# Loading attention keys through GpSimd's DMA queue, with the cast to float16 made by the transfer

## The chip, the cores and the metric

One core of one Trainium2 chip runs the kernel. The metric is the device time of one execution in microseconds (us); lower is better. The engines are named as the profile names them: PE (TensorE, matrix work; PEld is its weight load), DVE (VectorE), ACT (ScalarE), POOL (GpSimd) and SP (SyncE, which here only issues transfers).

## The reference, cut to what matters

Retention over 8 batches and 8 heads, sequences of 576, head width 64, followed by one feed-forward layer with a gated soft maximum and a normalisation. Inputs and outputs are float32.

```python
scores = scale * np.matmul(q, k.transpose(0, 1, 3, 2))
gamma = 1.0 - 2.0 ** (-5.0 - np.arange(H))
Dmat = np.where(rel >= 0, gamma[:, None, None] ** rel[None], 0.0)
x = np.matmul(scores * Dmat[None], v)        # then heads side by side: 4608 x 512

h = x @ w_in                                 # 4608 x 1024
solu = h * softmax(h)
ln = (solu - mean(solu)) / np.sqrt(var(solu) + 1e-06) * g_ln
out = ln @ w_out                             # 4608 x 512
```

## The kernel before, in words

*Tiling.* The 4608 rows are cut into 36 chunks of 128 rows. Two batches make a group of nine chunks: four of 128 rows of each batch, in turn, and one "tail" that holds the last 64 rows of both (lines 124 to 129; `rows`, line 131). There are four such groups. A chunk has its q, k and v for all eight heads, a tile of 128 x 8 x 64 each.

*Steps of a chunk.* Each is a short function whose name stands in the order. `ld` (line 168) loads q, k and v from memory as float32, on SP's queue: one transfer each of 256 KB, or two of 128 KB for a tail. A transfer gathers runs of 64 elements (256 B), one for each row and head. `cq` and `cv` multiply q and v by powers of gamma and write float16 (`scaled`, line 179). `ck` (line 190) casts the keys to float16 without scaling. For chunks under 15 and for tails `tq` (line 198) transposes q and k on PE; for the others q goes through PE (`tr`, line 217) and k through a transposing transfer on SP's queue (`kd`, line 209, issued at 213). `eq` and `er` copy the transposed tiles out of PSUM. `sc` forms the scores (line 247), `mk` masks them (DVE, line 265), `kv` multiplies keys by values (line 276) and is the last to read the float16 keys, `ad` adds that to the running state (DVE, lines 289 and 291), `dk` and `d3` scale the state to float16 and float32 for the next chunk (POOL, lines 303 and 315), `av` and `fs` form the retention's output (lines 327 and 342), `ex` copies it to float16. The second half is `m1` (first layer, line 374), `mx`, `xp`, `so` (maximum, exponential, gated product: lines 384, 390, 399), `sq` and `rt` (sum of squares on ACT, and the inverse root on POOL in three small instructions, lines 439 to 449), `tu` and `eu` (transpose and copy), `m2` (second layer, line 472) and `st` (ACT scales by the root, line 480, and SP stores, line 485).

*Order.* It is written out by hand. Every engine works through its own instructions in the order in which the steps stand in three lists: START (chunks' first steps, weight loads and weight casts), LOOP, run for i from 7 to 31 with steps at offsets from chunk i, and END. A letter at the end of a step names its engine: g for POOL, v for DVE, a for ACT. A transfer stands in the order of the queue that issues it. In LOOP POOL's steps are, in order, `dk:0`, `cv:3`, `rt:-2`, `cq:4`, `d3:0` and `ck:5`; `ld:6` stands ahead of `dk:0`, and `kd:4` between `dk:0` and `cv:3`. The loop's `ld` therefore covers chunks 13 to 35; START holds those of chunks 0 to 12 (in the order 0, 1, 2, 4, 3, 5 and on). Of the 36 key casts 29 are POOL's, 6 ACT's and 1 DVE's.

*Buffers.* The float32 tiles rotate through 6 buffers for keys and 7 each for q and v, the float16 keys through 6, float16 q and v through 5 each. A step that writes a buffer waits until the last reader of its former content is done.

Of the kernel before, what the change touches and what calls it, by code (L numbers as in the profile page):

```python
# [10 lines left out]
FP = mybir.dt.float32  # L11
F16 = mybir.dt.float16
BF16 = mybir.dt.bfloat16
P = 128
H = 8
D = 64
# [73 lines left out]
def kernel(  # L90
# [10 lines left out]
    nc = tc.nc  # L101
# [11 lines left out]
    load = ctx.enter_context(tc.tile_pool(name="load", bufs=6))  # L113
    half = ctx.enter_context(tc.tile_pool(name="half", bufs=4))
# [16 lines left out]
    def rows(n):  # L131

        bs, c = chunks[n]
        if c < 4:
            return [(slice(0, P), bs[0], c * P)]
        return [(slice(64 * i, 64 * i + 64), b, 4 * P) for i, b in enumerate(bs)]
# [24 lines left out]
    ENG = {"a": nc.scalar, "v": nc.vector, "g": nc.gpsimd}  # L161
    T = {}

    def copy(engine, out, in_):
        (engine.copy if engine is nc.scalar else engine.tensor_copy)(out=out, in_=in_)  # L165


    def ld(n):

        for key, src in (("qf", q), ("kf", k), ("vf", v)):  # L170
            dst = load.tile([P, H, D], FP, name=key, bufs=6 if key == "kf" else 7)
            for pp, b, s0 in rows(n):
                m = pp.stop - pp.start
                nc.sync.dma_start(  # L174
                    out=dst[pp], in_=src[b, :, s0 : s0 + m, :].rearrange("h p d -> p h d")
                )
            T[key, n] = dst
# [10 lines left out]
        scaled(n, "qf", "q16", gqt if chunks[n][1] == 4 else gq, ENG[e])  # L188

    def ck(n, e="g"):  # L190
        k16 = half.tile([P, H, D], F16, name="k16", bufs=6)
        copy(ENG[e], k16, T.pop(("kf", n)))
        T["k16", n] = k16

    def cv(n, e="g"):
        scaled(n, "vf", "v16", gkt if chunks[n][1] == 4 else gk, ENG[e])
# [520 lines left out]
```

## Time and profile before

| What | Value |
|---|---|
| Median of 2 runs | 221.14 us (220.74 to 221.54) |
| The profiled execution's own time | 220.91 us |
| Its span in the profile | 219.1 us |
| Granted PE clock | 0.996 |
| POOL key casts (line 165) | 29, 18.3 us busy, 629 ns mean |
| ACT key casts | 6, 626 ns mean |
| Key loads | 32 of 256 KB, 4.9 us to landing; 8 of 128 KB, 3.7 us |
| Transposing transfers of keys | 18, 3.8 us to landing |
| Data read from memory | 32.70 MB |

The span runs from the first to the last record; the execution's time is a little longer. "Busy" is the time in which an engine has an instruction in work; register, branch and transfer-issuing instructions are not counted in it. In the 40 slices a digit is the busy share of one slice in tenths. The DMA share is the mean busy share of the core's 16 DMA engines. In the table of windows the columns are: the stretch, its length, the busy time of PE, PEld, DVE, ACT and POOL with the number of their instructions, the granted PE clock, the DMA share and GB/s.

### The profile page before, as it was taken

The numbers are of one execution on the slowest core, as the hardware profiler recorded it, in microseconds if no ns is written. First come the engines' busy times: TensorE is split into PE (matmuls) and PEld (weight loads), VectorE is DVE, ScalarE is ACT, GpSimd is POOL, SyncE is SP. The second block draws the span as 40 slices with busy tenths as digits, with TensorE's granted clock in tenths as the row PEclk, the third lists the DMA queues.
The fourth block names the chain that finished last, engine by engine and source line by source line (L and its number), as shares of the span: only waits on it lengthen the run. The fifth ranks groups of instructions, "written<-read, shape, count | busy, mean of one in ns | idle before, by whom it ended". The sixth has DMA issues, their size and how long they took to land.

```text
span 219.1 us, 5479 instructions
## 1 busy us (share of the span) xinstructions
PE 200.1 (91%) x2060; PEld 114.3 (52%) x2060; DVE 174.4 (80%) x285; ACT 170.6 (78%) x274; POOL 174.5 (80%) x272
## 2 busy tenths in 40 slices
PE   1259889999989999999999999999999999999993
PEld 0235455555545555555555555555555555555552
DVE  1178999999997888888877788888878888889940
ACT  2064797989878888888888888888887888897992
POOL 0319899699796899999987899999988999994321
PEclk9999999999999999999999999999999999999998
DMA  7999999999999996799999998899999996610124
GB/s 143 236 282 314 206 221 355 225 203 231 278 279 215 252 205 140 176 253 209 235 236 220 230 219 180 195 247 232 226 226 230 211 226 146 161 51 15 37 97 144
DMA packets 130875, 44.86 MB, mean 205 GB/s; under 512 B 124448, under 2 KB 124832, under 8 KB 130848
## 3 DMA queue, kind: packets, MB, share of 16 engines
q1 hardware_dynamic: 129216, 44.18, 92.1%
q10 hardware_dynamic: 1632, 0.32, 0.9%
q8 instruction: 16, 0.26, 0.6%
q14 instruction: 11, 0.09, 0.2%
HBM read 32.70 MB, written 9.44 MB: 192 GB/s over the span
## 4 chain that ended last, share of the span: by engine, by line
PE 70%; DVE 12%; SPq 12%; DMA 2%; issue 2%; POOL 1%; DVEq 0%; POOLq 0%
PE o L472 24%; PE h L374 21%; SPq L174 10%; PE lp L457 6%; PE sc L252 4%; PE x L342 3%; PE x L327 3%; PE kp L276 3%; DMA qf<-in_q_dram 2%; DVE u L399 2%; DVE nm L384 2%; DVE w_c L669 2%; PE tr L223 2%; DVE ret L265 2%; PE tp L204 2%
## 5 line engine op out<-in xcount | busy, mean ns | idle before, releaser
L374 PE MATMUL h<-w_in,xT 128*128 128x512 f16 x264 | 62.4, 379 | 0.5 <-DVE u L399 0.5
L472 PE MATMUL o<-w_c,uT 128*128 128x512 f16 x232 | 54.6, 379 | 0.2
L390 ACT ACTIVATE e<-h,nm 128x1024 f32<-128x1024 f32 x35 | 39.1, 1116 | 12.5 <-DVE nm L384 12.5
L265 DVE TENSOR_TENSOR ret<-sc,tris 128x512 f16<-128x512 f32 x72 | 46.0, 680 | 0.6 <-PE sc L252 0.6
L399 DVE SCALAR_TENSOR_TENSOR u<-h,e 128x1024 f16<-128x1024 f32 x35 | 42.7, 1220 | 2.5 <-ACT e L390 0.9
L384 DVE TENSOR_REDUCE nm<-h 128x1 f32<-128x1024 f32 x35 | 42.3, 1214 | 1.4 <-PE h L374 1.1
L472 PEld LDWEIGHTS <-uT 128*128 128x128 f16 x280 | 26.1, 98 | 26.3
L374 PEld LDWEIGHTS <-xT 128*128 128x128 f16 x264 | 24.3, 98 | 24.2 <-issue 0.5
L303 POOL TENSOR_TENSOR s<-t,small 128x512 f16<-128x512 f32 x32 | 34.0, 1062 | 3.5 <-DVE t L291 3.5
L181 POOL TENSOR_TENSOR v<-vf,small 128x512 f16<-128x512 f32 x32 | 33.4, 1045 | 3.0 <-DMA vf<-in_v_dram 2.9
L181 POOL TENSOR_TENSOR q<-qf,small 128x512 f16<-128x512 f32 x32 | 33.4, 1044 | 2.8 <-DMA qf<-in_q_dram 2.8
L427 ACT ACTIVATE sq<-u,su 128x1024 bf16<-128x1024 f16 x29 | 33.6, 1159 | 1.0 <-DVE u L399 1.0
L165 ACT CAST xT<-x 128x512 f16<-128x512 f32 x35 | 20.5, 587 | 14.4 <-PE x L342 14.0
L165 ACT COPY uT<-lp 128x1024 f16<-128x1024 f16 x29 | 29.3, 1012 | 0.7 <-PE lp L457 0.4
L480 ACT ACTIVATE o_sb<-o,rs 128x512 f32<-128x512 f32 x35 | 23.8, 683 | 1.0 <-POOL q L181 0.8
L165 POOL CAST k<-kf 128x512 f16<-128x512 f32 x29 | 18.3, 629 | 6.1 <-DMA kf<-in_k_dram 6.1
L449 POOL TENSOR_TENSOR rs<-w,mhalf 128x1 f32<-128x1 f32 x36 | 19.9, 553 | 3.0
L291 DVE TENSOR_TENSOR t<-kp,s 128x256 f32<-128x256 f32 x24 | 10.1, 421 | 15.0 <-POOL s L303 11.8
L457 PE MATMUL lp<-ident,u 128*128 128x128 f16 x280 | 21.3, 219 | 0.7 <-DVE u L415 0.7
L445 POOL TENSOR_SCALAR w<-ss,w 128x1 f32<-128x1 f32 x30 | 8.0, 267 | 13.7 <-ACT sq L427 11.5
L457 PEld LDWEIGHTS <-u 128*128 128x128 f16 x280 | 17.2, 98 | 2.1 <-DVE u L415 0.8
L165 ACT COPY qkT<-tp 128x1024 f16<-128x1024 f16 x10 | 10.0, 1012 | 10.0 <-PE tp L204 10.0
(78 smaller groups left out, 266.3 us busy)
## 6 DMA issues: line engine op xcount, KB each, us to landing
qf<-in_q_dram SPq DMA_DIRECT2D x32, 256.0 KB, 4.4
kf<-in_k_dram SPq DMA_DIRECT2D x32, 256.0 KB, 4.9
vf<-in_v_dram SPq DMA_DIRECT2D x32, 256.0 KB, 4.9
out_dram<-o_sb SPq DMA_DIRECT2D x32, 256.0 KB, 2.9
w_in<-in_moe_w_in_dram SPq DMA_DIRECT2D x4, 512.0 KB, 5.2
w_out<-in_moe_w_out_dram SPq DMA_DIRECT2D x4, 512.0 KB, 6.3
qf<-in_q_dram SPq DMA_DIRECT2D x8, 128.0 KB, 3.4
kf<-in_k_dram SPq DMA_DIRECT2D x8, 128.0 KB, 3.7
```

Source lines behind the costliest of these rows:

```text
L165: (engine.copy if engine is nc.scalar else engine.tensor_copy)(out=out, in_=in_)
L181: engine.tensor_tensor(out=dst, in0=T.pop((key, n)), in1=table.unsqueeze(2).to_broadcast([P, H, D]), op=ALU.mult,)
L265: nc.vector.tensor_tensor(out=r, in0=s, in1=m, op=ALU.mult)
L303: nc.gpsimd.tensor_tensor(out=s16, in0=t.unsqueeze(2).to_broadcast([P, 4, 2, D]), in1=gd.unsqueeze(3).to_broadcast([P, 4, 2, D]), op=ALU.mult,
L374: nc.tensor.matmul(out=h[:, i * 512 : (i + 1) * 512], lhsT=xT[:, d], rhs=w_in16[:, d, i * 512 : (i + 1) * 512], start=d == 0, stop=d == 3,)
L384: nc.vector.tensor_reduce(out=nm, in_=T["h", n], axis=AX.X, op=ALU.max, negate=True)
L390: nc.scalar.activation(out=e, in_=T["h", n], func=ACT.Exp, bias=T.pop(("nm", n)), accum_out=s)
L399: nc.vector.scalar_tensor_tensor(out=u, in0=T.pop(("h", n)), scalar=-1.0, in1=T.pop(("e", n)), op0=ALU.mult, op1=ALU.mult, accum_out=su,)
L427: nc.scalar.activation(out=s, in_=T.pop(("v", n)), func=ACT.Square, scale=-float(DFF), bias=T.pop(("su", n)), accum_out=ss,)
L457: nc.tensor.transpose(out=lp[:, c], in_=u[:, c * P : (c + 1) * P], identity=ident)
L472: nc.tensor.matmul(out=o, lhsT=uT[:, c], rhs=w[:, c], start=c == 0, stop=c == NF - 1)
L480: nc.scalar.activation(out=o_sb, in_=T.pop(("o", n)), func=ACT.Copy, scale=T.pop(("rs", n)))
```

## The change

The keys are loaded by transfers that POOL issues, with a float16 tile as the destination: the transfer itself casts. `ld` stands in the three lists where it stood, so POOL issues a chunk's key load at the place of `ld` in its own order, and SP issues q and v. The float32 key tiles fall away, and `ck` only hands the tile on: it issues nothing. The float16 keys have 14 buffers in place of 6. The orders themselves are the same.

```diff
@@ def ld(n): @@
         for key, src in (("qf", q), ("kf", k), ("vf", v)):
-            dst = load.tile([P, H, D], FP, name=key, bufs=6 if key == "kf" else 7)
+            if key == "kf":
+                dst = half.tile([P, H, D], F16, name="k16", bufs=14)
+                queue = nc.gpsimd
+            else:
+                dst = load.tile([P, H, D], FP, name=key, bufs=7)
+                queue = nc.sync
             for pp, b, s0 in rows(n):
                 m = pp.stop - pp.start
-                nc.sync.dma_start(
+                queue.dma_start(
                     out=dst[pp], in_=src[b, :, s0 : s0 + m, :].rearrange("h p d -> p h d")
                 )
             T[key, n] = dst
@@ def ck(n, e="g"): @@
-        k16 = half.tile([P, H, D], F16, name="k16", bufs=6)
-        copy(ENG[e], k16, T.pop(("kf", n)))
-        T["k16", n] = k16
+        T["k16", n] = T.pop(("kf", n))
```

## The prediction

> **What bounds the kernel now.** I read the page first: busy shares, then the slices.
>
> ```profile
> PE 200.1 (91%) x2060; PEld 114.3 (52%) x2060; DVE 174.4 (80%) x285; ACT 170.6 (78%) x274; POOL 174.5 (80%) x272
> ...
> PE   1259889999989999999999999999999999999993
> ...
> POOL 0319899699796899999987899999988999994321
> ```
>
> PE is full from a third of the way on, POOL nearly so. The table of windows splits this (PE and POOL busy, the DMA share, GB/s at the end).
>
> ```profile
> 0.00:27.00 27.00, 14.76 (x145) 8.74 (x146) 14.93 (x27) 10.76 (x16) 12.36 (x21) 1.00 1.09 236
> 27.00:40.00 13.00, 11.49 (x158) 7.37 (x156) 12.38 (x21) 11.13 (x18) 10.80 (x13) 1.00 1.20 291
> 40.00:62.00 22.00, 21.22 (x176) 11.13 (x175) 21.89 (x39) 19.86 (x32) 19.50 (x29) 1.00 1.05 230
> 120.00:150.00 30.00, 29.97 (x325) 16.97 (x323) 24.68 (x41) 25.12 (x42) 28.36 (x45) 1.00 1.07 220
> ```
>
> Before 27 us no engine is full and transfers set the pace; up to 62 us DVE does; after it PE is busy 29.97 of 30 us. The chain of waits agrees: SP's issues up to 27 us, DVE's work from 34.9 to 62, PE's from there on. In it the first-layer matmul (line 374) starts at 65.85 and at 186.96 with 23 steps between, 121.1 us or 5.27 us a step.
>
> What matters for this change is how little POOL has to spare beside that PE. Its timeline in one full step, start and duration first:
>
> ```profile
> 130.93 1.04 POOL L181 TENSOR_TENSOR v<-vf,small 128x512 f16<-128x512 f32 x1
> 131.95 0.27 POOL L439 TENSOR_SCALAR w<-s 128x1 f32<-128x1 f32 x1
> 132.32 0.27 POOL L445 TENSOR_SCALAR w<-ss,w 128x1 f32<-128x1 f32 x1
> 132.67 0.55 POOL L449 TENSOR_TENSOR rs<-w,mhalf 128x1 f32<-128x1 f32 x1
> 133.19 1.04 POOL L181 TENSOR_TENSOR q<-qf,small 128x512 f16<-128x512 f32 x1
> 134.19 0.61 POOL L315 TENSOR_TENSOR s<-t,small 128x256 f32<-128x256 f32 x1
> 134.75 0.61 POOL L165 CAST k<-kf 128x512 f16<-128x512 f32 x1
> 135.32 1.04 POOL L303 TENSOR_TENSOR s<-t,small 128x512 f16<-128x512 f32 x1
> 136.32 1.04 POOL L181 TENSOR_TENSOR v<-vf,small 128x512 f16<-128x512 f32 x1
> ```
>
> From v to v it is 5.39 us with no wait shown. Start to start the parts are v 1.02, the root's three 1.24, q 1.00, s32 0.56, key cast 0.57, s16 1.00. In the 121.1 us there are 23 v, q and roots, 20 s16, 16 s32 and 22 casts: 23 x 3.26 + 20.0 + 9.0 + 12.5 = 116.5 us. POOL's slack is 4.6 us, 0.2 us a step.
>
> **The change, part by part.** Call X the time POOL spends on issuing one key load of 1024 runs of 256 B.
>
> *Removed casts.* 29 on POOL (0.57 us each), 6 on ACT (0.63), 1 on DVE (0.42). Those on ACT and DVE lie ahead of 62 us beside transfers or DVE's work; I cost them at nothing (below that, at most 4 us in all, if ACT were the bound there; at 19.86 of 22 us it isn't). Those in the loop give POOL 12.5 us, which alone shortens nothing since PE is full.
>
> *Added issues on POOL.* 36 chunks, 32 of one DMA and 4 of two halves (64 partitions each): 40 instructions. In START 13 chunks are loaded, seven of them (0 to 6) queued ahead of what POOL does at 22.8 us, six (7 to 12) after it; the loop loads the other 23, three of them in halves. In the loop the load stands after s32 and ahead of s16, where the cast stood, so X takes the place of 0.57 us: no other step changes its place. Behind it on POOL is s16, for which PE's state matmuls (line 342) wait in the same step, then v, the root (ACT's output scaling waits for it, line 480) and q.
>
> No row shows X. Lower end: SP issues the same load in 0.43 us when nothing holds it. Upper end: POOL's two-input loop takes 1045 ns for 512 elements, 2.04 ns a turn; 1024 reads and then 1024 writes listed one after the other at that rate are 4.2 us. The list is made by POOL's software, so I take the row nearest to it, POOL's simplest loop: the cast's 611 ns for 512 elements is 1.19 ns a turn, 1024 turns are 1.22 us, and one small instruction (0.2 us, line 443) makes X = 1.42; a pair of halves is X + 0.2.
>
> *Loop.* 116.5 - 12.5 + 23 X + 0.6 = 104.6 + 23 X against 121.1: growth 23 X - 16.5, from X = 0.72 on. At 1.42 it is 16.2 us. When POOL is late, s16 is late next, and PE stands still ahead of its state matmuls.
>
> *From 27 to 62 us.* POOL is busy 30.3 of 35 us, 4.7 free. Six chunks' loads, 6 X + 0.2, less two casts (1.1): growth 6 X - 5.6 where positive, 2.9 us at 1.42. DVE, the bound there, waits for POOL's states (lines 289 to 291), so I count it in full; the lower end is 0.
>
> *Up to 27 us.* 7 X less three casts (1.7) in 14.6 us free: growth 7 X - 16.3, nothing at 1.42.
>
> *SP's queue.* 40 issues leave. In the loop it waits for others anyway (30.1 us for ACT's output tiles alone), so nothing there. On the chain before 27 us the key loads are six pieces: 0.57 + 2.25 + 0.78 + 0.91 + 2.52 + 0.91 = 7.9 us. Between 0 and -7.9 I take 0: the packets are still carried, by engines whose share is 1.09 in that window, and the pieces of 2 us and more are waits for them.
>
> *The transfers.* Keys keep their reads; 128 B instead of 256 B are written per run. The queue's line:
>
> ```profile
> q1 hardware_dynamic: 129216, 44.18, 92.1%
> ```
>
> Keys are 36 x 1024 = 36,864 of these packets, 28.5%. If a casting packet took twice the time on engines that are full, the 121.1 us would grow by 34.5. Lower end 0, since less written can't help where PE is the bound. I take 0: the same engines carried 236 and 291 GB/s in the first two windows, and 220 in the loop.
>
> *Added waits.* The key tiles' 14 buffers: the load of chunk n reuses that of n - 14, whose last reader (line 276) ran many steps earlier; no wait. The transposing DMA of keys (line 213) waits for the landing instead of the cast. Its load was issued two steps earlier, 10.5 us, and key loads land after 4.9 us: 5.6 us of cover. Without it SP would stand still with q, v and stores queued behind, and each us of delay past the cover would come back as late q for POOL.
>
> *Contention.* POOL's rows in the loop have the same duration in every step (1.04, 0.61), with DVE at 82%: nothing stretches them. If each load waited for DVE's one wide copy of a step (420 ns, line 165 from PSUM), it would be 23 x 0.42 = 9.7 us more; if none, 0, which I take. The Trainium skill (SBUF — State Buffer, section SBUF: two separate sides, its box on the "DVE blocks DMA" trap) speaks against the change here: POOL can't write descriptors while DVE runs in a mode that takes both ports. By that rule the sum would be 249.4 if the copy is such an instruction; the steady rows don't show such a lock on POOL's own work.
>
> **The sum.** Span 219.1 + 16.2 + 2.9 = 238.2. The profiled execution took 220.91, 1.8 more than its span; so 240.0 us, against a median of 221.14 of two runs, which the profiled one stands 0.2 below.
>
> **The rivals.**
> *Cheap issue.* X under 0.91: the growth (23 X - 16.5) stays within 4.4 us, 2%, which is about what a measurement can tell from no change. PE still sets the loop, and the time is 221 to 225. For it: SP's 0.43 us. Against it: POOL's software loops are the dearest per element in the groups. The Trainium skill (DMA: Bandwidth & Descriptors, section Anatomy of one DMA — SWDGE (gpsimd) path) calls descriptor generation small and says that many can be emitted before the cost shows; by that the sum stays at 221. No run here shows it.
> *Dear issue.* X over 2.3: 23 X - 16.5 + 6 X - 5.6 + 7 X - 16.3; at 2.3 that is 36.4 + 8.2 = 44.6, 265.5 us; at 3.2 it is 57.1 + 13.6 + 6.1, 297.7; at 4.2, 80.1 + 19.6 + 13.1, 333.7. For it: two lists. Against it: two-input work is not what POOL has here.
> *Casting transfers become the bound.* 220.9 + 34.5 = 255.4 with packets of twice the time and a cheap issue. For it: shares of 1.0 to 1.1. Against it: the GB/s above.
> *Faster.* SP's 7.9 us of key issues leave the chain, and q and v land earlier: 213.0. It decides if X is under 0.72 and if issuing, not carrying, paces the first 27 us. Against it: the share of 1.09 there.
> That the keys are not cast on the way is not possible: the tile has another type than the source.
>
> **How the numbers follow.** Forecast (X from 0.91 to 2.3, 225 to 266, likeliest 240.0): 0.46. Dear issue 0.16, transfers 0.10, cheap issue 0.20, faster 0.08. So slower by over 2% 0.72, within 0.20, faster 0.08. The range is 219 to 297: it leaves out the fast case (0.08) and X over 3.2 (0.08).
>
> **What would show it.** Right: POOL without gaps from 62 us on with key loads of 1.2 to 1.6 us between s32 and s16, PE's idle before line 342 or 252 put down to POOL, steps near 5.95 us. Cheap: steps of 5.27 us and POOL with 0.2 us or more free. Transfers: SP's issues of q and v lengthen and POOL waits for qf. Faster: line 374 starts its steady run well before 65.85. Wrong above all if X is not near 1.4, since each 0.1 us is worth 2.9 us.

## The result, and the profile after

The changed kernel takes 233.17 us (median of 232.63 and 233.71) against 221.14: 1.0535 times as long, with a 95% interval from 1.0495 to 1.0574. It is slower. (Executions of a kernel that lie over 1.5% above its fastest count as slow and are left out of such ratios.) The profiled execution took 233.71 us with a span of 231.9.

The page's busy line, two of the slices, the queues and the key loads' own group, after:

```profile
PE 204.9 (88%) x2060; PEld 116.3 (50%) x2060; DVE 179.6 (77%) x284; ACT 168.2 (73%) x268; POOL 194.3 (84%) x283
...
PE   1368787796999999999979999999979999999993
...
POOL 4359999999747999999999999999999999995411
...
q1 hardware_dynamic: 91712, 34.74, 70.7%
q0 software_dynamic: 37504, 4.72, 32.0%
...
L179 POOL DMA_DIRECT2D k<-in_k_dram x40 | 36.7, 917 | 0.8 <-POOLq L704 0.8
```

PE's row of nines has gaps now, and POOL's has hardly any. The issues count as POOL's busy time here: 36.7 us in place of 18.3 us of casts. A second queue carries the keys: 4.72 MB, half the bytes, as float16.

POOL's timeline in a full step of the loop (the root's three small instructions left out):

```profile
129.37 1.05 POOL L186 TENSOR_TENSOR v<-vf,small 128x512 f16<-128x512 f32 x1
...
131.65 1.04 POOL L186 TENSOR_TENSOR q<-qf,small 128x512 f16<-128x512 f32 x1
132.65 0.60 POOL L318 TENSOR_TENSOR s<-t,small 128x256 f32<-128x256 f32 x1
133.21 0.97 POOL L179 DMA_DIRECT2D k<-in_k_dram  x1
134.21 1.06 POOL L306 TENSOR_TENSOR s<-t,small 128x512 f16<-128x512 f32 x1
135.21 1.04 POOL L186 TENSOR_TENSOR v<-vf,small 128x512 f16<-128x512 f32 x1
```

X, the time POOL spends on issuing one key load, is 0.97 us, and start to start 1.00 us where the cast took 0.57. From v to v it is 5.84 us, 0.45 more than before, while PE needs 5.27. A tail's pair of halves, at 139.05, takes 1.45 us.

Where the time went is read from the starts of the 35 exponentials (ACT's line 390, after it 393), one for each row block, in both traces:

| Exponential (counted from 0) | Before, us | After, us | Later by |
|---|---|---|---|
| 3 | 36.89 | 36.94 | 0.05 |
| 4 | 45.00 | 48.12 | 3.12 |
| 6 | 56.98 | 64.54 | 7.56 |
| 7 | 63.74 | 70.63 | 6.89 |
| 14 | 101.64 | 108.53 | 6.89 |
| 16 | 111.97 | 120.84 | 8.87 |
| 25 | 159.09 | 171.16 | 12.07 |
| 34 | 205.55 | 218.27 | 12.72 |

Two losses: 6.9 us between 37 and 70 us, in START, and 5.8 us in the loop after that. The first 37 us have neither gained nor lost. In the loop the loss comes in jumps (14 to 16, 21 to 25): POOL falls 0.45 us behind in each full step until its lead is used up, and catches up in the tails. Who waits there is told by the waits of the changed kernel from 66 to 219 us (in all, times, longest):

```profile
ACT o_sb L483 <- POOL rs L452: 11.4, 11, 1.5
DVE t L294 <- POOL s L318: 10.4, 10, 1.4
```

Only the first of the two is new. Before, ACT never waits for the root in the loop, while DVE waits just as long for POOL's states (10.8 us for line 303 between 62 and 207 us) and nothing is lost by it.

START's loss shows first on DVE. Its centering of u in place (SBUF to SBUF, line 415, now 418), its scaling of q and the centering of w_out that follows, before:

```profile
37.54 1.25 DVE L415 TENSOR_SCALAR u<-u,nmu 128x1024 f16<-128x1024 f16 x1
...
46.10 0.68 DVE L181 TENSOR_TENSOR q<-qf,small 128x512 f16<-128x512 f32 x1
46.71 1.08 DVE L669 TENSOR_TENSOR w_c<-w_out,warm 128x512 f16<-128x512 f16 x3
```

and after:

```profile
38.31 2.90 DVE L418 TENSOR_SCALAR u<-u,nmu 128x1024 f16<-128x1024 f16 x1
...
50.82 2.20 DVE L186 TENSOR_TENSOR q<-qf,small 128x512 f16<-128x512 f32 x1
52.94 2.04 DVE L672 TENSOR_TENSOR w_c<-w_out,warm 128x512 f16<-128x512 f16 x3
```

POOL's timeline after, beside the first of these, shows what stood there in the meantime:

```profile
37.88 0.97 POOL L179 DMA_DIRECT2D k<-in_k_dram  x1
38.88 2.04 POOL L653 TENSOR_TENSOR w_out<-w_out,g 128x512 f16<-128x512 f32 x2
40.86 1.42 POOL L179 DMA_DIRECT2D k<-in_k_dram  x2
```

DVE's centering ends (41.21) just after POOL's two casts of w_out (40.92). Before, POOL's three casts of w_out (37.47, 39.95 and 41.38) each waited for w_out to land, 2.2 us in all, and these waits were pauses beside DVE. In the changed kernel SP issues w_out 1.3 us earlier (29.42 against 30.68), and POOL waits for none of it. So the pauses were closed by two things, POOL's issues and the earlier w_out, and no run separates them.

Then PE, which waits for the centered u, runs slower: the window from 40 to 62 us has a granted clock of 0.84, and the first-layer matmuls that start at 42.74 take 2.96 us instead of 1.89.

Who waits for whom from 27 to 71 us in the changed kernel: ACT waits 0.6 us once for POOL's s16, and that is the only wait for POOL. No engine but POOL itself (0.2 us, for a v) waits for a transfer. DVE is busy for 32.4 of the 35 us from 27 to 62: it stands inside its own instructions.

### The profile page after: what moved, and what is told of

It reads as the page before. It is cut to its first block, busy times and chain, and to the rows that moved or that the text cites. A ratio compares the mean times of both kernels' runs of the same rounds, so it can differ in the third digit from the quotient of the medians.

```text
span 231.9 us, 5465 instructions
## 1 busy us (share of the span) xinstructions
PE 204.9 (88%) x2060; PEld 116.3 (50%) x2060; DVE 179.6 (77%) x284; ACT 168.2 (73%) x268; POOL 194.3 (84%) x283
## 3 DMA queue, kind: packets, MB, share of 16 engines
q0 software_dynamic: 37504, 4.72, 32.0%
## 4 chain that ended last, share of the span: by engine, by line
PE 47%; POOL 22%; DVE 10%; DMA 7%; issue 7%; SPq 3%; ACT 3%; POOLq 0%; DVEq 0%
PE o L475 15%; PE h L377 15%; DMA vf<-in_v_dram 5%; PE lp L460 4%; POOL k L179 4%; POOL v L186 4%; POOL s L306 3%; POOL q L186 3%; POOL s L318 3%; DVE nm L387 3%; PE sc L255 2%; PE x L345 2%; DVE u L402 2%; POOL rs L452 2%; SPq L179 2%
## 5 line engine op out<-in xcount | busy, mean ns | idle before, releaser
L377 PE MATMUL h<-w_in,xT 128*128 128x512 f16 x264 | 65.0, 391 | 0.5 <-DVE u L402 0.5
L393 ACT ACTIVATE e<-h,nm 128x1024 f32<-128x1024 f32 x35 | 39.0, 1115 | 15.6 <-DVE nm L387 15.4
L377 PEld LDWEIGHTS <-xT 128*128 128x128 f16 x264 | 25.0, 100 | 25.5 <-issue 3.0
L179 POOL DMA_DIRECT2D k<-in_k_dram x40 | 36.7, 917 | 0.8 <-POOLq L704 0.8
L186 POOL TENSOR_TENSOR v<-vf,small 128x512 f16<-128x512 f32 x32 | 34.0, 1063 | 2.5 <-DMA vf<-in_v_dram 2.4
L483 ACT ACTIVATE o_sb<-o,rs 128x512 f32<-128x512 f32 x35 | 23.9, 686 | 13.2 <-POOL rs L452 11.4
L165 ACT CAST xT<-x 128x512 f16<-128x512 f32 x35 | 20.5, 585 | 10.5 <-PE x L345 8.7
L294 DVE TENSOR_TENSOR t<-kp,s 128x256 f32<-128x256 f32 x24 | 10.1, 422 | 17.3 <-POOL s L318 10.4
L255 PE MATMUL sc<-qkT 64*128 64x128 f16 x288 | 15.8, 225 | 5.0 <-ACT uT L165 2.3
```

The source lines that it names most:

```text
L179: queue.dma_start(out=dst[pp], in_=src[b, :, s0 : s0 + m, :].rearrange("h p d -> p h d"))
L186: engine.tensor_tensor(out=dst, in0=T.pop((key, n)), in1=table.unsqueeze(2).to_broadcast([P, H, D]), op=ALU.mult,)
L377: nc.tensor.matmul(out=h[:, i * 512 : (i + 1) * 512], lhsT=xT[:, d], rhs=w_in16[:, d, i * 512 : (i + 1) * 512], start=d == 0, stop=d == 3,)
L393: nc.scalar.activation(out=e, in_=T["h", n], func=ACT.Exp, bias=T.pop(("nm", n)), accum_out=s)
```

## The experiments

**How they are read.** Several of these kernels scatter from execution to execution (four of the first experiment took 225.8 to 233.2 us, while the kernel before stayed between 220.97 and 222.39 beside them), so the losses are also read from each profile, which is one execution: START's is how much later exponential 7 starts than before, the loop's is what is added until exponential 34. "DVE's 22" is the busy time of DVE's 22 instructions in START that go from SBUF to SBUF (centering, q, v, w_out, and the centering of w_out, lines 415, 181, 645 and 669 before), the time in which two of one kind overlap counted once. An instruction of these is called held where it takes longer than it does alone.

| Kernel | Median (lowest to highest), us | START loss | Loop loss | DVE's 22, us |
|---|---|---|---|---|
| before | 221.14 (220.74 to 221.54) | 0 | 0 | 14.9 |
| changed | 233.17 (232.63 to 233.71) | 6.9 | 5.8 | 19.6 |
| e1 START only | 231.00 (225.83 to 233.20) | 8.1 | 0.0 | 20.9 |
| e2 loop only | 227.60 (226.95 to 228.09) | 0.7 | 5.9 | 14.8 |
| e3 no cast by the transfer | 248.47 (one run) | 7.4 | 20.0 | 19.4 |
| e4 two loads later | 231.63 (229.22 to 233.86) | 7.0 | 5.8 | 17.7 |
| e5 filler on PE | 234.47 (233.42 to 238.73) | 6.7 | 5.9 | 21.5 |
| e7 pairs | 227.77 (227.44 to 228.36) | 6.1 | 0.8 | 15.5 |
| e8 pairs, w_out on ACT | 228.19 (227.89 to 228.50) | 6.6 | 0.8 | 15.4 |
| e10 START before, pairs in loop | 222.95 (222.18 to 226.86) | 0.3 | 0.8 | 14.6 |
| e11 w_out on ACT | 232.54 (232.13 to 233.28) | 6.3 | 5.8 | 18.7 |
| e12 before, POOL filled | 235.76 (233.13 to 236.77) | 15.5 | 0.2 | 13.2 |

The ratios to before, with their 95% intervals (none for e1 and e3): e2 1.0267 (1.0226 to 1.0307), e4 1.036 (1.0313 to 1.0408), e5 1.0566 (1.0509 to 1.0623), e7 1.0286 (1.0243 to 1.0328), e8 1.0302 (1.0271 to 1.0333), e10 1.0052 (1.0022 to 1.0082), e11 1.0478 (1.0433 to 1.0523), e12 1.0573 (1.0505 to 1.0641).

**e1 and e2: each half of the change alone.** In `ld` and `ck` the new way holds for some chunks only:

```diff
-            if key == "kf":
+            if key == "kf" and n < 13:        # e2: n >= 13
                 dst = half.tile([P, H, D], F16, name="k16", bufs=14)
                 queue = nc.gpsimd
+            elif key == "kf":
+                dst = load.tile([P, H, D], FP, name=key, bufs=6)
+                queue = nc.sync
```

> Chunks 0 to 12 (the START list) get their keys by POOL's casting transfers as in the changed kernel; chunks 13 to 35 (the loop) as before: SP loads float32, the cast is a step of its own. Theory (two separate losses, 7.0 us up to the loop and 5.8 us in it, as the starts of the exponential show them in the two traces): about 228 us, with the loop's steps at 5.27 us. Rival (one loss: POOL is behind from START on, or casting transfers slow all others): either under 224 or as slow as the changed kernel, 233.

> The reverse: chunks 0 to 12 as before, chunks 13 to 35 by POOL's casting transfers. Theory: POOL's time in the loop is the loss, 104.6 + 20 x 0.97 + 3 x 1.42 against 121.1 us gives 7.2 at most, so 227 to 228 us. Rival (POOL only falls behind because it enters the loop late; with a loop entered on time its buffers carry it): under 224 us.

e2 came to 227.6 us, as expected, and lost 5.9 us in the loop after entering it only 0.7 us late; e1 lost nothing at all in its loop, and its four executions lie on both sides of the 228 us expected. So the losses are separate and, within START's scatter, add up: 6.9 and 5.8 in the changed kernel, 8.1 and 0.0 in e1, 0.7 and 5.9 in e2. The rival that POOL is late in the loop only because it enters late has fallen.

**e3: the issue without the cast.** The 36 casts stay, and POOL issues plain float32 loads:

```diff
             if key == "kf":
-                dst = half.tile([P, H, D], F16, name="k16", bufs=14)
+                dst = load.tile([P, H, D], FP, name=key, bufs=6)
                 queue = nc.gpsimd
```

> POOL issues the key loads where the changed kernel does, but as plain float32 into float32 tiles, and the 36 key casts stay where they were before. Theory (POOL's time is the loss in the loop; the issue costs 0.97 us with or without a cast): POOL needs 116.5 + 20 x 0.97 + 3 x 1.42 = 140.2 us for the 23 steps against 121.1, so about 19 us lost in the loop, with START's loss about 247 us. Rival (it is the casting that makes the issue dear, a plain one costs 0.5 us): POOL needs 129 us, 236 us. Rival (casting transfers slow the others, not POOL): no more than 233 us.

248.47 us in its one execution, against 247 expected by the theory. POOL's timeline has the cast and, behind it, an issue at the same price as with casting:

```profile
152.40 0.60 POOL L165 CAST k<-kf 128x512 f16<-128x512 f32 x1
152.95 0.97 POOL L179 DMA_DIRECT2D kf<-in_k_dram  x1
153.95 1.05 POOL L308 TENSOR_TENSOR s<-t,small 128x512 f16<-128x512 f32 x1
```

By POOL's count the loop should lose 116.5 + 20 x 0.97 + 3 x 1.42 - 121.1 = 19.1 us; it lost 20.0. POOL's time is what the loop pays for, and casting has no part in the price.

**e6: the costs by themselves.** A kernel of its own, which leaves out all that the reference computes: DVE and POOL run short rows of the kernel's instructions, alone and side by side.

> No part of the reference is computed (the output is zeros): the disputed costs alone, in stretches that DVE and POOL start together. DVE runs rows of 10 centering steps (128x1024 float16, SBUF to SBUF), 8 scalings of q (two SBUF inputs), 8 copies from PSUM; first alone, then beside 8 casting key loads issued by POOL, then the first two beside 8 scalings by POOL; after that POOL issues key loads of 128, 256, 512 and 1024 runs with the cast and 1024 without. Theory: centering takes 0.49 us alone and about 1 us or more beside either kind of POOL work, scaling 0.68 and over 1.2 us, the copies from PSUM 0.68 in both; the issue takes 0.45 us and 0.5 us for each 1024 runs (0.51, 0.57, 0.70, 0.97). Rival on holding: DVE waits only for POOL's scalings, which read SBUF, and not for issues. Rival on the price: the issue costs the same for any number of runs, or less without the cast.

DVE's rows, in order: 10 centerings and 8 scalings alone, then beside 8 issues, then beside 8 scalings by POOL (8 copies from PSUM, left out here, took 4.87 us alone and 4.86 beside issues):

```profile
9.23 4.05 DVE L130 TENSOR_SCALAR u<-u,scal 128x1024 f16<-128x1024 f16 x10
13.83 4.90 DVE L135 TENSOR_TENSOR o<-qf,table 128x512 f16<-128x512 f32 x8
...
24.70 5.25 DVE L130 TENSOR_SCALAR u<-u,scal 128x1024 f16<-128x1024 f16 x10
33.67 4.90 DVE L135 TENSOR_TENSOR o<-qf,table 128x512 f16<-128x512 f32 x8
...
49.33 10.32 DVE L130 TENSOR_SCALAR u<-u,scal 128x1024 f16<-128x1024 f16 x10
60.21 10.82 DVE L135 TENSOR_TENSOR o<-qf,table 128x512 f16<-128x512 f32 x8
```

My theory had the issues hold DVE. For the most part they don't: beside them scalings and copies take what they take alone, and ten centerings 1.2 us more (0.78 us for four of them instead of 0.48). POOL's own scalings hold DVE: 2.5 and 2.2 times as long. The eight issues took 8.27 us beside the centerings and 7.01 beside the scalings, so there POOL waits a little too. The rival on holding was right, but for these 1.2 us.

The price of an issue, from the same kernel: 0.56 us for 128 runs (median of 4), 0.72 for 256, 0.77 for 512, 0.92 for 1024 with the cast and 0.91 without. Half a microsecond is fixed; eight times the runs add 0.36.

**e7 and e8: fewer issues.** Two chunks of the same rows in one load:

```diff
-            if key == "kf":
+            if key == "kf" and chunks[n][1] < 4:
+                m = n - n % 9 % 2
+                if (key, n) not in T:
+                    (b,), c = chunks[m]
+                    two = half.tile([P, 2 * H, D], F16, name="k16", bufs=7)
+                    nc.gpsimd.dma_start(
+                        out=two,
+                        in_=src[b : b + 2, :, c * P : (c + 1) * P, :].rearrange(
+                            "b h p d -> p (b h) d"
+                        ),
+                    )
+                    for i in range(2):
+                        T[key, m + i] = two[:, i * H : (i + 1) * H]
+                continue
```

and in e8 besides, in START, `wo:4:g wo:1:g wo:7:g` as `wo:4:a wo:1:a wo:7:a`.

> The changed kernel with one key load for two chunks (the same rows of both batches, 2048 runs, one tile of both; the tails stay). The number of runs is the same, the issues are 24 instead of 40. Theory (0.45 us for an issue and 0.5 us for 1024 runs): 1.45 us a pair, POOL saves 0.25 us a chunk in the loop, 104.6 + 10 x 1.45 + 3 x 1.42 = 123.4 against 121.1, so 2 us lost there instead of 5.9, and less of START's loss: 226 to 229 us. Rival (an issue costs by its runs alone): 1.94 us a pair, no gain, 232 us. Rival (an issue has one price): 0.97 us a pair, nothing lost in the loop.

> The pairs, and the three casts of w_out that POOL makes near 37 to 42 us given to ACT (0.73 us each), which has lost 3.6 us of key casts. Theory (START's loss is DVE held by a POOL without pauses): POOL has 3.1 us of pauses again in that stretch, and most of START's loss goes: 223 to 225 us. Rival (START's loss comes from the transfers or from a late q or v): as the pairs alone.

A pair costs 1.24 us:

```profile
L176 POOL DMA_DIRECT2D k<-in_k_dram x16 | 19.8, 1240 | 0.8 <-POOLq L718 0.8
```

POOL's count of the loop is 104.0 + 10 x 1.24 + 3 x 1.42 = 120.7 against 121.1, and 0.8 us are lost there. But 5.4 us of START's 6.1 are lost already when the first exponential starts (28.65 against 23.22 us): another place. In the first 30 us of e7 PE waits for keys, 9.0 us in two waits, the longest 5.4:

```profile
PE tp L221 <- DMA k<-in_k_dram: 9.0, 2, 5.4
```

In the changed kernel the same wait is 1.8 us in the whole span. As I read it, a pair's keys land only when both chunks have, and they share the engines with the q and v that are wanted first (POOL waits 9.7 us for q in these 30 us, 5.8 in the changed kernel). From the first exponential on e7 loses 0.6 us in START, with 15.5 us on DVE's 22 instructions. e8 is as late at the first exponential (5.0 us) and is no faster, and in e7 hardly anything was held, so e8 told nothing of w_out; e11 asks that again.

**e4 and e11: pauses for POOL near 38 us.** e4 moves the key loads of chunks 7 and 8 (`ld:7:qv`, `ld:8:qv` in place, `ld:7:k ld:8:k` behind `rt:1`; the expectation says ahead of this root, the kernel run has them behind it); e11 gives the three casts of w_out to ACT, as e8 did, with single loads.

> The changed kernel with the key loads of chunks 7 and 8 (three issues) moved on POOL's order from among the three casts of w_out to behind them, ahead of the root of chunk 1; q and v of these chunks stay. POOL's work up to 50 us is the same, but it has pauses again near 38 to 42 us. Theory (DVE's instructions that work from SBUF to SBUF can't start while POOL goes from one instruction to the next without a pause; at 38.31 one took 2.90 instead of 1.25 us): that instruction is under 1.5 us again and the exponential of the fifth and sixth row starts about 3 us earlier: 230 us. Rival (POOL's total work up to 50 us is what costs, wherever it stands): 233 us, no gain.

> The changed kernel (single loads) with the three casts of w_out that POOL makes near 37 to 42 us given to ACT; all loads where the change has them. Theory (START's loss is DVE held by POOL's own SBUF work, which the issues push together): the row that took 2.90 us takes under 1.3, about 3 us come back, 229 to 231 us. Rival (the loss is from the transfers): 233 us.

In both the long centering is short again: 1.08 us in e4, 0.65 in e11, where it took 2.90. In the table START's loss stays: 7.0 and 6.3 us. In e11 the time went to the next place. DVE's centering of w_out (three in a row; at this place 1.08 us in the kernel before and 2.04 in the changed one), in e11:

```profile
40.00 0.65 DVE L418 TENSOR_SCALAR u<-u,nmu 128x1024 f16<-128x1024 f16 x1
...
49.19 5.43 DVE L672 TENSOR_TENSOR w_c<-w_out,warm 128x512 f16<-128x512 f16 x3
```

and POOL beside it in e11, without a pause from 49.04 on:

```profile
49.04 0.97 POOL L179 DMA_DIRECT2D k<-in_k_dram  x1
50.03 1.06 POOL L306 TENSOR_TENSOR s<-t,small 128x512 f16<-128x512 f32 x1
51.02 0.94 POOL L179 DMA_DIRECT2D k<-in_k_dram  x1
51.98 1.06 POOL L186 TENSOR_TENSOR v<-vf,small 128x512 f16<-128x512 f32 x1
52.99 1.35 POOL L672 TENSOR_TENSOR w_c<-w_out,warm 128x512 f16<-128x512 f16 x1
```

What I said of the row held, what I said of the time didn't: 232.5 us, not 229 to 231. In e11, taking away one hold didn't take away the loss.

e4 is not decided. Two of its four executions took 229.22 and 229.91 us, as its theory had it, and two 233.35 and 233.86, as the rival had it; the profile is of the last. In that one START was lost in another way: from 40 to 64 us its chain of waits runs through POOL, and ACT waits 2.5 us for roots. What the two quicker executions did differently no trace shows.

**e9: issue and scaling in turn.** As e6, with POOL alternating.

> No part of the reference is computed (the output is zeros). In the measurement before, 8 key-load issues in a row left DVE's scalings at 0.61 us each, while 8 scalings by POOL made them 1.35 us. Here POOL alternates, issue and scaling, as in the kernel's START, beside 10 centerings and 8 scalings on DVE. Theory (an issue gives DVE its turn, POOL's own SBUF work holds it): DVE gets ahead during each issue, 8 scalings take 8 us or less, less than beside scalings alone (10.8 us). Rival (behind an issue POOL's next instruction already holds DVE): DVE waits through issue and scaling, about 2 us for each DVE instruction that meets them, 13 us or more.

Ten centerings took 12.61 us (10.32 beside scalings alone), eight scalings 11.35 (10.82):

```profile
42.44 12.61 DVE L130 TENSOR_SCALAR u<-u,scal 128x1024 f16<-128x1024 f16 x10
...
59.23 11.35 DVE L135 TENSOR_TENSOR o<-qf,table 128x512 f16<-128x512 f32 x8
```

Neither number was met (8 or less; 13 or more). The longest single scaling took 2.61 us, where beside scalings alone none took over 1.53: an issue that stands next to a scaling is often no turn for DVE, and sometimes DVE stands through a scaling and both issues around it. This goes the rival's way, with a smaller price. Not every issue fails DVE, though: two of the later scalings took 0.68 us.

**e5: is PE's slow clock on the path?** Eight idle matmuls on PE ahead of each of its two long stops:

```diff
-... tu:0 tu:2 ...
+... tu:0 fill:3:8 tu:2 ...
-... tq:8 ...
+... fill:3:8 tq:8 ...
```

> The changed kernel with 8 matmuls without use (1.7 us) put on PE ahead of each of the two places where it stood still for over 2 us (38.9 and 54.7 us). Theory (PE runs slower after standing still: granted clock 0.84 and 0.71, the first-layer matmuls at 42.7 and 57.4 take 2.96 and 3.43 instead of 1.89 us, and this is on the path): those rows are 1.9 us again and 2.6 us come back: 230.5 us. Rival (DVE alone sets the pace there, PE's slow rows are hidden): 233 us.

The granted clock from 40 to 62 us is 1.00 instead of 0.84 and the matmuls are 1.89 us again, but the time is 234.5 us. START's loss is 6.7 us, so the 230.5 us of the theory were not met, and a loss of this size needs no slow PE. What the slow rows cost in the changed kernel this doesn't tell: there they took 2.96 and 3.43 us, 2.6 us more than here, but here DVE's 22 took 1.9 us more than there. In e5's trace no engine waits for POOL or a transfer from 27 to 71 us, and the chain of waits from 36 to 69 us is DVE's alone; its 22 took 6.6 us more than before, and 6.7 were lost.

**e12: work on POOL without any transfer.** The kernel before, with fills of a small tile where the new loads 7 to 12 would stand, four for each and six for the tail:

```diff
+    def pf(_, count):
+        for _ in range(int(count)):
+            nc.gpsimd.memset(scratch, 0.0)
...
-... ld:7 ...
+... pf:0:4 ld:7 ...
```

> The kernel before, with all its keys loaded by SP and cast as before, and POOL given work without use where the changed kernel has the key loads of chunks 7 to 12: 4 fills of a small tile (6 for the tail), about 1.1 us, that read nothing and move no data. Theory (START's loss comes from POOL's pauses being filled, which holds DVE's SBUF work and makes POOL late; the casting transfers have no part in it): START loses 4 to 8 us here too, 225 to 229 us, and the loop keeps 5.27 us a step. Rival (the casting transfers or their place in the queues cause it): START loses under 2 us, less than 223.5 us.

The fills came out at 0.54 us each, twice what I had reckoned: 14.1 us in all instead of some 7, and against 6.3 us of issues in the changed kernel. START lost 15.5 us and the loop 0.2. So POOL's time alone can make a loss in START, with the keys on SP's queue; of that the rival had said under 2 us. The loss was larger than the theory's 4 to 8, with twice the work, and not by the road that I had named: fills read nothing, and DVE's 22 instructions took 13.2 us, less than before. There ACT stood 9.9 us for the root, DVE 9.1 us for the scores, and PE 3.8 us for a POOL cast of keys and 2.4 for its q: POOL was late. That is not what the changed kernel's trace shows, where nobody but ACT, for 0.6 us, waits for POOL in START. So e12 shows that such a loss needs no transfers; it doesn't show what made the changed kernel's.

**e10: the cheapest form of the change.** START as before, pairs in the loop.

> Chunks 0 to 12 as before the change, the loop with casting key loads for two chunks at a time (1.24 us each by the pairs' run). Theory (START's loss and the loop's are separate and add up, START by loop-only loads lost 0.7 us, pairs lost 1.0 us in the loop): 222.6 to 223 us, within 2% of before, and not faster, since PE sets the loop's pace at 5.27 us a step. Rival (taking casts and issues off POOL, ACT and SP is worth something once POOL keeps up): under 220 us.

222.95 us, 1.0052 times before: the sum of the two parts' losses, as expected: within 2% of before and, if anything, slower. PE is busy 29.97 of 30 us from 90 to 120 us. Freeing ACT, SP and POOL of casts and issues is worth nothing there.

## Why the prediction was right, and where it was wrong

*What bounds the kernel.* Right. PE sets the loop's pace, and POOL's slack of 4.6 us is all that the change could use. e10, with POOL's count under 121.1 us, loses 0.8 us; e3, with POOL's count at 140.2, loses 20.0 against 19.1.

*X.* Mis-sized: 1.42 us predicted, 0.97 measured, for a pair of halves 1.42 to 1.45 instead of 1.62. It lies between the two ends, but the row that I took as the nearest, a turn of POOL's loop for each run, was the wrong kind: an issue is half a microsecond and little for each run (0.56 us for 128, 0.92 for 1024, 1.24 for 2048). The Trainium skill (DMA: Bandwidth & Descriptors, section Anatomy of one DMA — SWDGE (gpsimd) path) says that many descriptors can be emitted before their cost shows; here it does show, 0.36 us from 128 runs to 1024, though it is the smaller part. The fixed half microsecond is about as much as the cast that it replaces.

*The loop.* The step was right and so was its formula: with the measured prices 104.0 + 20 x 0.97 + 3 x 1.42 - 121.1 = 6.6 us, against 5.8 in the changed kernel and 5.9 in e2. The 16.2 us on record were too much by X alone. The road to PE was only in part the one that I named. From 70 to 219 us PE itself waits 1.8 us (2 times) for s16 ahead of its state matmuls, and 2.3 us (6 times) ahead of the scores for ACT's copy of uT, which stands behind the output scaling and so behind POOL's root.

*From 27 to 62 us.* Here the prediction failed. Its formula at 0.97 gives 5 x 0.97 + 1.42 - 1.1 - 4.7 = 0.5 us; 6.9 were lost, all after 37 us. I took POOL's 4.7 us without work for room to be filled. They weren't free, and 2.2 of them were waits for w_out that went away with the change: DVE's 22 instructions from SBUF to SBUF ran in them. In the changed kernel these take 4.7 us more (19.6 against 14.9). The formula was about a POOL that comes late, and there is hardly a wait for POOL in that stretch (0.6 us); it was DVE's own instructions that were stretched, and behind them two groups of PE's matmuls ran 2.6 us longer at a lower granted clock. The two errors were of opposite sign: 10.4 us too much in the loop (16.2 for 5.8), 4.0 too little in START (2.9 for 6.9), and so 240.0 came near 233.2: that nearness is luck, while slower by POOL's time in the loop is not.

*Contention.* "0, which I take", from the loop's steady rows: true in the loop (e2's rows are as steady), wrong for START, where DVE works from SBUF. I had looked at what DVE does to POOL, and it was POOL that held DVE. The Trainium skill (SBUF — State Buffer, section Who interferes with whom) has this: a DVE instruction with two SBUF inputs contends with a GpSimd instruction that reads SBUF and not with one that only writes it, and the wait is for the whole instruction. The traces agree: scalings 2.2 times as long beside scalings in e6, as long as ever beside issues, and 0.68 us for the scaling that ran beside fills in e12. That the centering, with one tensor from SBUF, is held by POOL's scalings too (1.26 us for 0.48) and a little by issues is not in this rule. The box that I cited, DVE keeping POOL from its descriptors, shows only a little: 8.27 us for eight issues beside centerings, 7.01 beside scalings. (The 249.4 on record for it is a slip; 240.0 + 9.7 is 249.7.)

*Up to 27 us, and SP's queue.* Right at 0: exponential 0 starts 0.3 us earlier, exponential 3 0.05 us later. Taking 7.9 us of issues off SP's part of the chain gained nothing: the transfers set the pace there. e7 shows the other side of it, 5.4 us lost by fetching keys before they were wanted.

*The transfers.* Right at 0 in the loop, by e3 and e10. A casting packet takes longer, though: in the trace of the changed kernel the 36,864 of them (128 B written) take 32.0 ns of one engine on average, plain packets of 256 B 21.7 beside them and 20.7 in the kernel before; so about 1.5 times, not twice.

*The removed casts* on ACT and DVE were worth nothing, as costed. *Added waits*: none of the transposing loads waited for keys (keys land after 5.4 us of 10.5 available).

*The rivals.* Dear issue and faster: out. Cheap issue: X missed its bound (0.91) by a little, and START would have decided against it in any case. Transfers as the bound: out.

*What stays open.* How START's 6.9 us divide between DVE's stretched instructions (4.7 us) and PE's slow matmuls behind them (2.6 us in the changed kernel, none in e5); the two overlap. That the stretching is the cause is read from the chains of waits and from e6; no run takes the holds away and leaves the rest. How much of it is due to POOL's issues and how much to the earlier w_out is open too. e11 took away the longest and the next grew, e4 scattered, and e12 lost time by the other road, a late POOL. That START with pairs loses early but not late (e7, 15.5 us on DVE's 22) speaks for the holds, and was not tried apart from the early loss.

## What to carry to other kernels

Before work is put on an engine, count its time per step against the step of the engine that sets the pace: here 0.43 us more in each full step, with 0.2 us to spare, was the whole loss of the loop. A pause of an engine that shares a way to memory with another is that other's time to run, so look at who works in it before filling it. A transfer that saves a cast was paid here by POOL's issue, and mostly at a fixed price: few large issues, and none ahead of what is wanted first.

## What the runs showed of the hardware that had not been expected

- POOL's issue of a key load costs 0.56 us for 128 runs of 256 B, 0.92 for 1024 and 1.24 for 2048, the same with and without a cast.
- POOL's scalings from SBUF make DVE's centerings 1.26 us instead of 0.48, and its scalings 1.52 instead of 0.68 (medians). POOL's issues in a row leave the scalings as they are and make some centerings 0.78; beside its fills in e12 a scaling took 0.68, one centering 0.49 and one 0.86.
- An issue next to a scaling is no sure pause for DVE: single DVE instructions took up to 2.73 us in e9.
- A POOL fill of 128x512 float16 took 0.54 us on average, hardly less than its cast from float32 (0.61).
- A packet of a casting load occupies its DMA engine for 32.0 ns, a plain packet of 256 B for 21.7 beside it.
